# An adaLN block of cached attention and a gated MLP: loading order, first chunk and row stride of V changed

## The chip, the cores and the metric

One core of one Trainium2 chip runs the whole program. The metric is the time of one execution on the device in microseconds (us); a kernel's figure is the median of its runs. The profile comes from one execution, recorded instruction by instruction. The engines are called TensorE (PE for matmuls, PEld for weight loads), VectorE (DVE), ScalarE (ACT), GpSimd (POOL) and SyncE (SP, which here only issues DMAs). Each takes its instructions in the order in which the program issues them.

## The reference

Inputs are bfloat16: `x` (1, 2048, 512), a key and a value cache of 8 heads with 2048 rows of 128, 32 query heads (four to each key head), a spatial gating MLP of width 1792, and a modulation vector `c`.

```python
mod = (silu(c) @ w_mod).reshape(1, 6, 1, 512)
sa, ca, ga, sb, cb, gb = mod[:, 0], ..., mod[:, 5]
h = layernorm(x) * (1 + ca) + sa
q = (h @ wq) in 32 heads of 128
p = softmax(q k^T * 128 ** -0.5);  o = p v          # 4 query heads share a k/v head
x = x + ga * (o @ wo)
h = layernorm(x) * (1 + cb) + sb
z = gelu(h @ w_in);  z1, z2 = z[..., :896], layernorm(z[..., 896:])
g = w_sp @ z2 + b_sp                                # over the 2048 positions
x = x + gb * ((z1 * g) @ w_out)
```

## The kernel before

The order of all work is written out by hand: every engine gets its instructions in the order in which the Python code issues them, and waits are put in where data or a buffer asks for it. The function is `tile_adaLN_cond__gqa_block_cached__mixer_gmlp__prompt_kernel`.

**Units and slots.** Attention is cut into 128 units: unit u is key head u // 16 and query tile u % 16 (128 positions, four query heads, so 512 columns). The main loop runs over `it` (one unit each) and eight slots in it. In a slot `qk(it, i)` does two QK matmuls of 512 columns (L879) into a two-bank tile `s_ps`, and ScalarE makes the exponential of it, 1024 wide (L886). `pv(it - 1, i)` does eight PV matmuls of 129 columns (L901) for the unit before: 128 columns of V and a column of ones, which gives the softmax's sum. After slots 3 and 7 VectorE takes the reciprocal (L912) and scales (L913, `onorm`). Three units later `wo_proj` adds the output projection (L933) in slots 4 to 7, with a VectorE copy or add into `xacc` at the end.

**Order inside a slot.** First whatever was entered with `at(it, slot, fn)` into `later`, then `qk`, then `pv`, then the matmuls in `fill[it, slot]`, then one `wo_proj` matmul.

**Banks.** PSUM pools have two buffers of each name: `s_ps` (two banks each), `o_ps` (for PV and the modulation columns) and `misc` (one bank each; for query projections, output projections, transposes of layer-norm tiles, and the rows of the modulation). A buffer is given out again when the last user of its tile is done; a tile whose accumulation is still open keeps its buffer.

**Chunks.** Four tiles make a chunk of 512 positions. Before a chunk's queries can be projected, `ln1_stats` takes mean and variance of each tile on VectorE (L690, L691) and the reciprocal root on GpSimd (L671, L675), `ln1_norm` normalises (L679, VectorE), and `ln1_turn` transposes on TensorE (L796) in two halves, each into one `misc` bank, and evicts with scale and shift into `hT` (L803, VectorE). `qproj` multiplies with the query weights (L843) and casts into `qT` (L852, VectorE). `set_fill(b)` spreads the 16 projection matmuls of block b (a chunk for a key head) over slots.

**The beginning.** SyncE issues loads in the order c, tile 0 of x, the first third of `w_mod` (`wmod_a`), K of head 0, tiles 1 to 3 of x, the query weights of head 0, V of head 0, x tiles 4 to 7, the rest of `w_mod`, x tiles 8 to 15, `wo`, `w_in`. Then tile 0 is normalised, `mod_columns` makes shift and scale (L759), tile 0 is turned, K is transposed on TensorE (L821, 16 transposes) and copied by ScalarE in two halves (L825), and the queries of tile 0 are projected. Tiles 1 to 3 are normalised together (L829, L861), turned together at slot 0 of unit 0 and projected head by head with 384 columns over unit 0's eight slots (L1026 to L1029).

**Later chunks.** `ln1_at(it, ch)` enters chunk ch's statistics at slot 1, its normalisation at slot 5 and its turn at slot 7 of unit it: units 0, 2 and 5 for chunks 1, 2 and 3. `mod_rest` (L990) makes the other modulation columns and the gate rows (L1002) at slot 0 of unit 3. The projection of block 1 is spread over slots 0 to 7 of units 1 and 2, one matmul a slot; that of each later block over slots 0 to 3 of four units.

**V.** `load_v` puts V into tiles `v1` of 16 rows with `DV = DH + 8` = 136 elements each (272 bytes); the DMA writes 128 of them, GpSimd sets the others to one (L712), PV reads 129. The same `DV` sets the distance of the two heads in the `o_ps` bank.

Of the kernel before, what the change touches and what calls it, by code (L numbers as in the profile page):

```python
# [10 lines left out]
BF16 = mybir.dt.bfloat16  # L11
# [4 lines left out]
P = 128  # L16
# [559 lines left out]
def kernel(  # L576
# [19 lines left out]
    nc = tc.nc  # L596
    _, S, D = A_x.shape
    _, HKV, SK, DH = A_k_cache.shape
    HQ = A_wq.shape[1] // DH
    REP = HQ // HKV  # L600
# [5 lines left out]
    NDT = D // P  # L606
    NKT = SK // P
    NFT = FH // P
    NCH = S // 512
    CT = 512 // P  # L610
    FC = _f_chunk(FH)
    NFHC = FH // FC
    NSLOT = NKT // 2
    DV = DH + 8
    inv_sqrt_dh = 1.0 / math.sqrt(DH)

    NB = HKV * NCH
    x_dram = A_x[0].rearrange("(t p) d -> p t d", p=P)
# [4 lines left out]
    k_rows = A_k_cache[0].rearrange("g (p t) d -> p g t d", p=P)  # L623
# [18 lines left out]
    late = free_b.enter_context(tc.tile_pool(name="late", bufs=2, side="right"))  # L642
    early = free_a.enter_context(tc.tile_pool(name="early", bufs=2))

    x_sb = res.tile([P, NT, D], BF16, name="x_sb")
# [13 lines left out]
    ident = res.tile([P, P], BF16, name="ident")  # L659
    ones_bf = res.tile([P, P], BF16, name="ones_bf")  # L660

    def bank(name):
        return psum.tile([P, 512], FP32, name=name)

    def bank2():
        return psum.tile([P, 1024], FP32, name="s_ps")
# [28 lines left out]
    nc.sync.dma_start(out=c_bf[:], in_=c_dram)  # L695
    nc.sync.dma_start(out=x_sb[:, 0, :], in_=x_dram[:, 0, :])
    nc.sync.dma_start(out=wmod_a[:], in_=wmod_dram[:, :, 0 : 2 * D])
    k_nat = early.tile([P, SK], BF16, name="kT")
    nc.sync.dma_start(out=k_nat[:].rearrange("p (t d) -> p t d", d=DH), in_=k_rows[:, 0])
    nc.sync.dma_start(out=x_sb[:, 1:CT, :], in_=x_dram[:, 1:CT, :])  # L700

    groups, wqs, hTs, qTs = {}, {}, {}, {}

    def load_wq(g, engine):
        wqs[g] = early.tile([P, NDT, REP * DH], BF16, name="wq_g")
        engine.dma_start(
            out=wqs[g][:], in_=wq_dram[:, :, g * REP * DH : (g + 1) * REP * DH]
        )

    def load_v(g, rows, engine):  # L710
        v1 = late.tile([P, NKT, DV], BF16, name="v1")
        nc.gpsimd.memset(v1[:, :, DH:DV], 1.0)  # L712
        engine.dma_start(out=v1[:, :, 0:DH], in_=rows[:, g])
        groups[g]["v1"] = v1
# [11 lines left out]
    nc.gpsimd.memset(mhalf[:], -0.5)  # L726
    make_identity(nc, ident[:])
    load_wq(0, nc.sync)
    groups[0] = {}
    load_v(0, v_rows, nc.sync)  # L730
    nc.sync.dma_start(out=x_sb[:, CT : 2 * CT, :], in_=x_dram[:, CT : 2 * CT, :])
# [2 lines left out]
    load_wo(0, nc.sync)  # L734
    nc.sync.dma_start(out=win_sb[:], in_=win_dram)


    c_f = res.tile([P, NDT], FP32, name="c_f")
    nc.vector.tensor_copy(out=c_f[:], in_=c_bf[:])
# [6 lines left out]
    nc.vector.tensor_tensor(out=sc[:], in0=c_f[:], in1=sig[:], op=ALU.mult)  # L746
    sc_bf = res.tile([P, NDT], BF16, name="sc_bf")
    nc.vector.tensor_copy(out=sc_bf[:], in_=sc[:])
    nc.vector.memset(ones_bf[:], 1.0)

    def mod_columns(first, wmod, i0):

        mc_ps = bank("o_ps")
        for i in range(2):
            for dt in range(NDT):
                col = i * NDT + dt
                w0 = (first + i - i0) * D + dt * P
                for kt in range(NDT):
                    nc.tensor.matmul(  # L759
                        mc_ps[:, col : col + 1],  # L760
                        lhsT=wmod[:, kt, w0 : w0 + P],
                        rhs=sc_bf[:, kt : kt + 1],
                        start=(kt == 0),
                        stop=(kt == NDT - 1),
                    )
        c0 = first * NDT
        nc.vector.tensor_copy(out=modc[:, c0 : c0 + NDT], in_=mc_ps[:, 0:NDT])
        nc.vector.tensor_scalar_add(
            out=modc[:, c0 + NDT : c0 + 2 * NDT], in0=mc_ps[:, NDT : 2 * NDT], scalar1=1.0
        )  # L770


    def ln1_stats(j0, n):
        for j in range(j0, j0 + n):
            ln_stats(mv1, j, x_sb[:, j, :])
        return rstd_of(mv1[:, j0 : j0 + n, :], n, "ln1")

    def ln1_norm(j0, n, rstd):
        xns = []
        for j in range(j0, j0 + n):  # L780
            xn = res.tile([P, D], BF16, name="xn1", bufs=4)
            normalise(xn[:], x_sb[:, j, :], mv1[:, j, 0:1], rstd[:, j - j0 : j - j0 + 1])
            xns.append(xn)
        return xns

    def ln1_turn(j0, n, xns):
        ch, c0 = j0 // CT, (j0 % CT) * P
        if ch not in hTs:
            hTs[ch] = res.tile([P, NDT, 512], BF16, name="hT", bufs=NCH)
        hT = hTs[ch]  # L790
        for half in range(2):
            t_ps = bank("misc")[:].bitcast(BF16).rearrange("p (k q) -> p k q", k=2)
            for k in range(2):
                dt = half * 2 + k
                for jj in range(n):
                    nc.tensor.transpose(  # L796
                        t_ps[:, k, jj * P : (jj + 1) * P],
                        xns[jj][:, dt * P : (dt + 1) * P],
                        ident[:],
                    )  # L800
            for k in range(2):
                dt = half * 2 + k
                nc.vector.tensor_scalar(  # L803
                    out=hT[:, dt, c0 : c0 + n * P],
                    in0=t_ps[:, k, 0 : n * P],
                    scalar1=modc[:, NDT + dt : NDT + dt + 1],
                    scalar2=modc[:, dt : dt + 1],
                    op0=ALU.mult,
                    op1=ALU.add,
                )  # L810

    xns0 = ln1_norm(0, 1, ln1_stats(0, 1))
    mod_columns(0, wmod_a, 0)
    ln1_turn(0, 1, xns0)


    kT0 = early.tile([P, SK], BF16, name="kT")
    groups[0]["kT"] = kT0
    k_ps = bank2()[:].bitcast(BF16)
    for kt in range(NKT):  # L820
        nc.tensor.transpose(  # L821
            k_ps[:, kt * P : (kt + 1) * P], k_nat[:, kt * P : (kt + 1) * P], ident[:]
        )
    for hf in range(2):
        nc.scalar.copy(  # L825
            out=kT0[:, hf * SK // 2 : (hf + 1) * SK // 2],
            in_=k_ps[:, hf * SK // 2 : (hf + 1) * SK // 2],
        )
    rstd0 = ln1_stats(1, CT - 1)  # L829

    def qproj(b, heads, c0, n):

        g, ch = divmod(b, NCH)
        if b not in qTs:
            qTs[b] = early.tile([P, REP, 512], BF16, name="qT")
        one = n * len(heads) <= 512
        ps = {}

        def mm(hh, dt):
            if dt == 0 and (not one or hh == heads[0]):  # L840
                ps[0] = bank("misc")
            o0 = (hh - heads[0]) * n if one else 0
            nc.tensor.matmul(  # L843
                ps[0][:, o0 : o0 + n],
                lhsT=wqs[g][:, dt, hh * DH : (hh + 1) * DH],
                rhs=hTs[ch][:, dt, c0 : c0 + n],
                start=(dt == 0),
                stop=(dt == NDT - 1),
            )
            if dt == NDT - 1 and (not one or hh == heads[-1]):  # L850
                hs = heads if one else [hh]
                nc.vector.tensor_copy(  # L852
                    out=qTs[b][:, hs[0] : hs[-1] + 1, c0 : c0 + n],
                    in_=ps[0][:, 0 : len(hs) * n].rearrange("p (h q) -> p h q", q=n),
                )

        return [lambda hh=hh, dt=dt: mm(hh, dt) for hh in heads for dt in range(NDT)]

    for fn in qproj(0, list(range(REP)), 0, P):
        fn()  # L860
    xns0 = ln1_norm(1, CT - 1, rstd0)  # L861


    NU = HKV * NT
# [3 lines left out]
    def at(it, slot, fn):  # L868
        later.setdefault((it, slot), []).append(fn)
# [23 lines left out]
    def pv(u, i):  # L893
# [3 lines left out]
        if i % (2 * per) == 0:  # L897
            o_pss[u] = bank("o_ps")[:, 0 : 2 * DV].rearrange("p (h d) -> p h d", h=2)
        o_ps = o_pss[u]
# [116 lines left out]

    wsp = [None] * NCH

    def ln1_at(it, ch):
        st = {}  # L1020
        at(it, 1, lambda: st.update(r=ln1_stats(ch * CT, CT)))
        at(it, 5, lambda: st.update(x=ln1_norm(ch * CT, CT, st["r"])))
        at(it, 7, lambda: ln1_turn(ch * CT, CT, st["x"]))

    fill = {}
    rest0 = qproj(0, list(range(REP)), P, 512 - P)  # L1026
    at(0, 0, lambda: ln1_turn(1, CT - 1, xns0))
    for i in range(NSLOT):
        fill[0, i] = rest0[2 * i : 2 * i + 2]  # L1029
    ln1_at(0, 1)  # L1030
    ln1_at(2, 2)
    ln1_at(5, 3)
    at(3, 0, mod_rest)

    def set_fill(b):

        fs = qproj(b, list(range(REP)), 0, 512)
        for k, fn in enumerate(fs):
            it, slot = ((b - 1) * CT + k // NDT, k % NDT) if b > 1 else (1 + k // 8, k % 8)
            fill.setdefault((it, slot), []).append(fn)  # L1040

    def wsp0():
# [5 lines left out]
    for g in range(1, HKV):  # L1048
        it = (g - 1) * NT + 4
# [122 lines left out]
    for f in range(NFT):  # L1172
# [6 lines left out]
        out=ok1[:], in0=rall[:], scalar1=1.0 / SAFE, scalar2=None, op0=ALU.is_ge  # L1179
# [8 lines left out]
        out=bad[:], in0=okm[:], scalar1=-1.0, scalar2=1.0, op0=ALU.mult, op1=ALU.add  # L1188
# [133 lines left out]
```

## Time and profile before

| | us |
|---|---|
| median of three runs | 1346.97 (1346.54 to 1347.03) |
| the profiled execution | 1347.03 |
| its span, first to last instruction | 1345.2 |
| TensorE busy | 1303.1 (97%) |
| ScalarE busy | 1079.2 (80%) |
| VectorE busy | 476.3 (35%) |
| GpSimd busy | 46.4 (3%) |
| granted TensorE clock, mean over the span | 0.996 |

A row of the profile's groups gives line, engine, operation, what is written from what, the shapes, the count, then busy time in all with the mean length of one in ns, then the idle time of the engine ahead of it with what ended most of it. A row of the timeline gives start, length, engine, line, operation and, in brackets, idle time and its releaser. Two rows of the load times in the first 30 us: the query weights of head 0 landed 7.9 us after their issue at 3.28, and K 6.3 us after its issue at 2.26. VectorE's share is an average: in the first 45 us it runs short chains that other engines wait for.

### The profile page before, as it was taken

How to read it: one execution, taken by the hardware profiler on the slowest of the kernel's cores; microseconds unless marked ns; L12 is line 12 of the kernel's file. 1: busy time of each engine (PE TensorE's matmuls, PEld its weight loads, DVE VectorE, ACT ScalarE, POOL GpSimd, SP SyncE). 2: the span in 40 equal slices, each digit the busy share in tenths (PEclk: the TensorE clock that was granted, in tenths of full speed). 3: DMA queues.
4: the chain of work that ended last, by engine and by line, in shares of the span. 5: the costliest groups of instructions: out<-in, count | busy, mean ns of one | idle time of the engine just before them, and what ended most of it. 6: DMA issues, size and time to landing. Idle time of an engine off the chain costs nothing.

```text
span 1345.2 us, 27642 instructions
## 1 busy us (share of the span) xinstructions
PE 1303.1 (97%) x12137; PEld 860.4 (64%) x12345; DVE 476.3 (35%) x1171; ACT 1079.2 (80%) x1059; POOL 46.4 (3%) x88
## 2 busy tenths in 40 slices
PE   6999999999999999999999999999999999979997
PEld 4666666666666666666666666666666666534444
DVE  5442222222222222222222222222222666873344
ACT  4789999999999999999999999999999999540000
POOL 1010000000000000000000000000000000110000
PEclk9999999999999999999999999999999999989999
DMA  8120021102211120012010410121111111143200
GB/s 274 29 64 17 13 63 37 21 17 35 62 20 21 32 68 17 17 37 68 17 20 13 84 21 17 21 64 32 21 20 17 29 29 33 25 110 83 67 20 26
DMA packets 141184, 56.53 MB, mean 42 GB/s; under 512 B 131105, under 2 KB 136353, under 8 KB 141057
## 3 DMA queue, kind: packets, MB, share of 16 engines
q1 hardware_dynamic: 137504, 42.17, 15.0%
q0 software_dynamic: 3408, 12.45, 3.5%
q8 instruction: 98, 1.61, 0.5%
q14 instruction: 30, 0.24, 0.1%
q10 hardware_dynamic: 144, 0.07, 0.0%
HBM read 21.63 MB, written 2.10 MB: 18 GB/s over the span
## 4 chain that ended last, share of the span: by engine, by line
PE 92%; DVE 3%; SPq 2%; issue 1%; DMA 1%; POOL 0%; ACT 0%; ACTq 0%; POOLq 0%; DVEq 0%
PE s_ps L879 35%; PE o_ps L901 34%; PE misc L843 7%; PE misc L933 6%; PE misc L1205 6%; PE s_ps L1100 2%; SPq L1012 1%; PE o_ps L1220 1%; PE s_ps L1064 1%; DMA wq_g<-in_A_wq_dram 1%; DVE stz L1081 1%; DVE hT L803 0%; PE s_ps L1220 0%; PE misc L796 0%; DVE bnst L690 0%
## 5 line engine op out<-in xcount | busy, mean ns | idle before, releaser
L886 ACT ACTIVATE pT<-s_ps 128x1024 bf16<-128x1024 f32 x1024 | 1045.6, 1024 | 92.2 <-PE s_ps L879 16.5
L901 PEld LDWEIGHTS <-pT 128*128 128x128 bf16 x8192 | 548.5, 98 | 241.2
L901 PE MATMUL o_ps<-v,pT 128*128 128x129 bf16 x8192 | 631.4, 220 | 0.0
L879 PE MATMUL s_ps<-qT,kT 128*128 128x512 bf16 x2048 | 609.9, 379 | 10.8 <-DVE qT L852 0.8
L912 DVE RECIPROCAL rall<-o_ps 128x2 f32<-128x2 f32 x256 | 43.6, 170 | 750.9 <-PE o_ps L901 750.7
L879 PEld LDWEIGHTS <-kT 128*128 128x128 bf16 x2048 | 199.8, 98 | 120.1 <-issue 1.3
L843 PE MATMUL misc<-hT,wq_g 128*128 128x512 bf16 (+2 forms) x462 | 169.1, 376 | 0.8 <-DMA wq_g<-in_A_wq_dram 0.8
L933 PE MATMUL misc<-wo_g,oT 128*128 128x512 bf16 x386 | 146.3, 379 | 0.0
L913 DVE TENSOR_TENSOR onorm<-o_ps,rall 128x256 bf16<-128x256 f32 x256 | 108.7, 425 | 8.8
L1205 PE MATMUL misc<-wsp,z 128*128 128x512 bf16 (+2 forms) x555 | 100.5, 336 | 1.8 <-DVE gb L1214 1.3
L852 DVE CAST qT<-misc 128x512 bf16<-128x512 f32 (+1 forms) x129 | 87.2, 676 | 1.0 <-PE misc L843 1.0
L1205 PEld LDWEIGHTS <-z 128*128 128x128 bf16 x560 | 50.7, 98 | 50.3 <-issue 1.8
L946 DVE TENSOR_TENSOR xacc<-misc,xacc 128x512 f32<-128x512 f32 x112 | 76.2, 680 | 0.0
L843 PEld LDWEIGHTS <-wq_g 128*128 128x128 bf16 x528 | 51.8, 99 | 3.6 <-DMA wq_g<-in_A_wq_dram 1.0
L933 PEld LDWEIGHTS <-oT 128*128 128x128 bf16 x512 | 50.1, 98 | 0.7
L1214 DVE TENSOR_TENSOR gb<-misc,bsp_bc 128x512 bf16<-128x512 f32 (+2 forms) x35 | 20.4, 584 | 60.9 <-PE misc L1205 60.9
L1100 PE MATMUL s_ps<-hT,win_sb 128*128 128x512 bf16 x109 | 26.5, 401 | 7.3 <-ACT z1T L1108 7.1
L1108 ACT ACTIVATE z1T<-s_ps 128x1024 bf16<-128x1024 f32 x14 | 14.2, 1024 | 19.5 <-PE s_ps L1100 10.9
L1064 PE MATMUL s_ps<-win_sb,hT 128*128 128x448 bf16 x128 | 27.0, 352 | 0.1
L1074 ACT ACTIVATE z<-s_ps 128x896 bf16<-128x896 f32 x16 | 14.7, 917 | 14.9 <-PE s_ps L1064 14.9
L712 POOL MEMSET v<- 128x128 bf16 x8 | 1.6, 205 | 705.9 <-issue 606.9
L1100 PEld LDWEIGHTS <-win_sb 128*128 128x128 bf16 x112 | 11.5, 102 | 21.9 <-issue 10.1
(68 smaller groups left out, 288.6 us busy)
## 6 DMA issues: line engine op xcount, KB each, us to landing
v<-in_A_v_cache_dram POOLq DMA_DIRECT2D x7, 512.0 KB, 6.6
wo_g<-in_A_wo_dram POOLq DMA_DIRECT2D x7, 512.0 KB, 4.8
wq_g<-in_A_wq_dram POOLq DMA_DIRECT2D x7, 512.0 KB, 6.0
wsp<-in_w_mod_dram SPq DMA_DIRECT2D x1, 2048.0 KB, 9.2
oT<-onorm SPq DMA_TRANSPOSE x128, 2.4
out_dram<-yout SPq DMA_DIRECT2D x15, 128.0 KB, 1.7
win_sb<-in_B_w_in_dram SPq DMA_DIRECT2D x1, 1792.0 KB, 13.6
wmod_a<-in_w_mod_dram SPq DMA_DIRECT2D x1, 1024.0 KB, 5.4
```

The source lines that it names most:

```text
L843: nc.tensor.matmul(ps[0][:, o0 : o0 + n], lhsT=wqs[g][:, dt, hh * DH : (hh + 1) * DH], rhs=hTs[ch][:, dt, c0 : c0 + n], start=(dt == 0), s ...
L852: nc.vector.tensor_copy(out=qTs[b][:, hs[0] : hs[-1] + 1, c0 : c0 + n], in_=ps[0][:, 0 : len(hs) * n].rearrange("p (h q) -> p h q", q=n),)
L879: nc.tensor.matmul(s_ps[:, h * 512 : (h + 1) * 512].rearrange("p (r q) -> p r q", r=REP), lhsT=groups[g]["kT"][:, kt * P : (kt + 1) * P], ...
L886: nc.scalar.activation(out=pTs[u][:, 2 * i : 2 * i + 2, :], in_=s_ps[:].rearrange("p (k q) -> p k q", k=2), func=ACT.Exp, scale=inv_sqrt_dh,)
L901: nc.tensor.matmul(o_ps[:, hh % 2, 0 : DH + 1], lhsT=pTs[u][:, kt, hh * P : (hh + 1) * P], rhs=groups[g]["v1"][:, kt, 0 : DH + 1], start=( ...
L912: nc.vector.reciprocal(out=rall[:, c0 : c0 + 2], in_=o_ps[:, :, DH])
L913: nc.vector.tensor_tensor(out=onorms[u][:, hh - 1 : hh + 1, :], in0=o_ps[:, :, 0:DH], in1=rall[:, c0 : c0 + 2].unsqueeze(2).to_broadcast([ ...
L933: nc.tensor.matmul(X_ps[:], lhsT=oTs[u][:, hh, :], rhs=groups[g]["wo"][:, hh, :], start=(hh == 0), stop=(hh == REP - 1),)
L946: nc.vector.tensor_tensor(out=xaccs[j][:], in0=X_ps[:], in1=xaccs[j][:], op=ALU.add)
L1064: nc.tensor.matmul(ps[0][:, hf * 512 : hf * 512 + FC], lhsT=h2Ts[j // CT][:, dt, (j % CT) * P : (j % CT + 1) * P], rhs=win_sb[:, dt, FH + ...
L1100: nc.tensor.matmul(ps[0][:, k * 512 : (k + 1) * 512], lhsT=win_sb[:, dt, f * P : (f + 1) * P], rhs=h2Ts[2 * ch2 + k][:, dt, :], start=(dt ...
L1205: nc.tensor.matmul(g_ps[:, :n], lhsT=z2[:, st, f * P : (f + 1) * P], rhs=wsp[t][:, st, c0 : c0 + n], start=(st == 0), stop=(st == NT - 1),)
```

## The change

Five things are edited.

1. The loads: the query weights go ahead of K; K is loaded in two halves; tiles 1 to 3 of x follow them.
2. Idle matmuls: VectorE clears a tile of zeros first thing, and `warm(n)` issues n matmuls of 512 columns on it whose result nobody reads: 18 before the modulation columns, 3 behind them, 4 before the first query projection.
3. The first chunk: K's transposes and copies come after tile 0's query projection, in halves. Tiles 1, 2 and 3 are each handled by themselves, in units 0, 1 and 2: statistics at slot 0, normalisation at slot 1, turn at slot 2, and 16 projection matmuls of 128 columns, four in each of slots 4 to 7.
4. Later chunks: statistics at slot 4, normalisation at slot 7, turn at slot 0 of the next unit; `mod_rest` moves from slot 0 to slot 3 of unit 3; block 1's projection starts at slot 4 of unit 1 and ends at slot 3 of unit 3.
5. V's rows: `DV` is 130 in place of 136, so 260 bytes from row to row.

```diff
@@ -611,7 +611,7 @@
     FC = _f_chunk(FH)
     NFHC = FH // FC
     NSLOT = NKT // 2
-    DV = DH + 8
+    DV = DH + 2
     inv_sqrt_dh = 1.0 / math.sqrt(DH)
 
     NB = HKV * NCH
@@ -695,10 +695,6 @@
     nc.sync.dma_start(out=c_bf[:], in_=c_dram)
     nc.sync.dma_start(out=x_sb[:, 0, :], in_=x_dram[:, 0, :])
     nc.sync.dma_start(out=wmod_a[:], in_=wmod_dram[:, :, 0 : 2 * D])
-    k_nat = early.tile([P, SK], BF16, name="kT")
-    nc.sync.dma_start(out=k_nat[:].rearrange("p (t d) -> p t d", d=DH), in_=k_rows[:, 0])
-    nc.sync.dma_start(out=x_sb[:, 1:CT, :], in_=x_dram[:, 1:CT, :])
-
     groups, wqs, hTs, qTs = {}, {}, {}, {}
 
     def load_wq(g, engine):
@@ -726,6 +722,14 @@
     nc.gpsimd.memset(mhalf[:], -0.5)
     make_identity(nc, ident[:])
     load_wq(0, nc.sync)
+    k_nat = early.tile([P, SK], BF16, name="kT")
+    hk = NKT // 2
+    for hf in range(2):
+        nc.sync.dma_start(
+            out=k_nat[:, hf * SK // 2 : (hf + 1) * SK // 2].rearrange("p (t d) -> p t d", d=DH),
+            in_=k_rows[:, 0, hf * hk : (hf + 1) * hk],
+        )
+    nc.sync.dma_start(out=x_sb[:, 1:CT, :], in_=x_dram[:, 1:CT, :])
     groups[0] = {}
     load_v(0, v_rows, nc.sync)
     nc.sync.dma_start(out=x_sb[:, CT : 2 * CT, :], in_=x_dram[:, CT : 2 * CT, :])
@@ -734,6 +738,11 @@
     load_wo(0, nc.sync)
     nc.sync.dma_start(out=win_sb[:], in_=win_dram)
 
+
+
+    zeros = late.tile([P, REP, DH], BF16, name="onorm", bufs=3)
+    nc.vector.memset(zeros[:], 0.0)
+    nc.vector.memset(ones_bf[:], 1.0)
 
     c_f = res.tile([P, NDT], FP32, name="c_f")
     nc.vector.tensor_copy(out=c_f[:], in_=c_bf[:])
@@ -746,7 +755,15 @@
     nc.vector.tensor_tensor(out=sc[:], in0=c_f[:], in1=sig[:], op=ALU.mult)
     sc_bf = res.tile([P, NDT], BF16, name="sc_bf")
     nc.vector.tensor_copy(out=sc_bf[:], in_=sc[:])
-    nc.vector.memset(ones_bf[:], 1.0)
+
+    def warm(n):
+        w_ps = bank2()
+        for k in range(n):
+            nc.tensor.matmul(
+                w_ps[:, 0:512].rearrange("p (r d) -> p r d", r=REP), lhsT=zeros[:, 0, :], rhs=zeros[:], start=True, stop=True
+            )
+
+    warm(18)
 
     def mod_columns(first, wmod, i0):
 
@@ -811,22 +828,8 @@
 
     xns0 = ln1_norm(0, 1, ln1_stats(0, 1))
     mod_columns(0, wmod_a, 0)
+    warm(3)
     ln1_turn(0, 1, xns0)
-
-
-    kT0 = early.tile([P, SK], BF16, name="kT")
-    groups[0]["kT"] = kT0
-    k_ps = bank2()[:].bitcast(BF16)
-    for kt in range(NKT):
-        nc.tensor.transpose(
-            k_ps[:, kt * P : (kt + 1) * P], k_nat[:, kt * P : (kt + 1) * P], ident[:]
-        )
-    for hf in range(2):
-        nc.scalar.copy(
-            out=kT0[:, hf * SK // 2 : (hf + 1) * SK // 2],
-            in_=k_ps[:, hf * SK // 2 : (hf + 1) * SK // 2],
-        )
-    rstd0 = ln1_stats(1, CT - 1)
 
     def qproj(b, heads, c0, n):
 
@@ -856,9 +859,21 @@
 
         return [lambda hh=hh, dt=dt: mm(hh, dt) for hh in heads for dt in range(NDT)]
 
+    warm(4)
     for fn in qproj(0, list(range(REP)), 0, P):
         fn()
-    xns0 = ln1_norm(1, CT - 1, rstd0)
+
+
+    kT0 = early.tile([P, SK], BF16, name="kT")
+    groups[0]["kT"] = kT0
+    k_ps = bank2()[:].bitcast(BF16)
+    for hf in range(2):
+        for kt in range(hf * hk, (hf + 1) * hk):
+            nc.tensor.transpose(
+                k_ps[:, kt * P : (kt + 1) * P], k_nat[:, kt * P : (kt + 1) * P], ident[:]
+            )
+        half = slice(hf * SK // 2, (hf + 1) * SK // 2)
+        nc.scalar.copy(out=kT0[:, half], in_=k_ps[:, half])
 
 
     NU = HKV * NT
@@ -1016,27 +1031,32 @@
 
     wsp = [None] * NCH
 
-    def ln1_at(it, ch):
+    fill = {}
+    for jj in range(1, CT):
+        st1 = {}
+        at(jj - 1, 0, lambda jj=jj, st1=st1: st1.update(r=ln1_stats(jj, 1)))
+        at(jj - 1, 1, lambda jj=jj, st1=st1: st1.update(x=ln1_norm(jj, 1, st1["r"])))
+        at(jj - 1, 2, lambda jj=jj, st1=st1: ln1_turn(jj, 1, st1["x"]))
+        rest = qproj(0, list(range(REP)), jj * P, P)
+        for k, fn in enumerate(rest):
+            fill.setdefault((jj - 1, 4 + k // 4), []).append(fn)
+
+    def ln1_at(it, slot, ch):
         st = {}
-        at(it, 1, lambda: st.update(r=ln1_stats(ch * CT, CT)))
-        at(it, 5, lambda: st.update(x=ln1_norm(ch * CT, CT, st["r"])))
-        at(it, 7, lambda: ln1_turn(ch * CT, CT, st["x"]))
-
-    fill = {}
-    rest0 = qproj(0, list(range(REP)), P, 512 - P)
-    at(0, 0, lambda: ln1_turn(1, CT - 1, xns0))
-    for i in range(NSLOT):
-        fill[0, i] = rest0[2 * i : 2 * i + 2]
-    ln1_at(0, 1)
-    ln1_at(2, 2)
-    ln1_at(5, 3)
-    at(3, 0, mod_rest)
+        at(it, slot, lambda: st.update(r=ln1_stats(ch * CT, CT)))
+        at(it, slot + 3, lambda: st.update(x=ln1_norm(ch * CT, CT, st["r"])))
+        at(it + 1, 0, lambda: ln1_turn(ch * CT, CT, st["x"]))
+
+    ln1_at(0, 4, 1)
+    ln1_at(2, 4, 2)
+    ln1_at(5, 4, 3)
+    at(3, 3, mod_rest)
 
     def set_fill(b):
 
         fs = qproj(b, list(range(REP)), 0, 512)
         for k, fn in enumerate(fs):
-            it, slot = ((b - 1) * CT + k // NDT, k % NDT) if b > 1 else (1 + k // 8, k % 8)
+            it, slot = ((b - 1) * CT + k // NDT, k % NDT) if b > 1 else (1 + (k + 4) // 8, (k + 4) % 8)
             fill.setdefault((it, slot), []).append(fn)
 
     def wsp0():
```

## The prediction

> **What bounds the kernel now.** I read four views: the page's groups of instructions, the busy time by stretches, the chain of waits over the first 80 us, and TensorE's timeline around the unit boundaries.
>
> ```profile
> L886 ACT ACTIVATE pT<-s_ps 128x1024 bf16<-128x1024 f32 x1024 | 1045.6, 1024 | 92.2 <-PE s_ps L879 16.5
> L901 PE MATMUL o_ps<-v,pT 128*128 128x129 bf16 x8192 | 631.4, 220 | 0.0
> L879 PE MATMUL s_ps<-qT,kT 128*128 128x512 bf16 x2048 | 609.9, 379 | 10.8 <-DVE qT L852 0.8
> ```
> ```profile
> 400.00:1100.00 700.00, 693.75 (x6877) 474.99 (x6996) 209.61 (x527) 651.05 (x637) 16.28 (x28) 1.00 0.16 32
> ```
>
> The second fence holds, behind the stretch and its length, the busy time of PE, PEld, DVE, ACT and POOL. TensorE is busy 693.75 of 700 us there, and nothing in the change shortens this part. What it can move is the beginning, and every idle moment of TensorE that it adds or takes away up to the last edited unit.
>
> ```profile
> 3.28 7.95 DMA wq_g<-in_A_wq_dram
> 11.23 0.05 issue
> 11.28 1.90 PE misc L843 x16
> ...
> 20.80 1.05 POOL rstd_ln L675
> 21.85 0.03 issue
> 21.88 1.38 DVE xn L679 x4
> 23.26 0.48 DVE qT L852
> ...
> 27.66 0.60 PE s_ps L879 x2
> ```
>
> Here the chain (start, length, what) shows the beginning waiting for the query weights, then for the statistics of chunk 1 (VectorE, then GpSimd, then VectorE), then for the last query cast. QK of unit 1 starts at 27.66.
>
> ```profile
> 43.96 0.38 PE L843 MATMUL misc<-hT,wq_g 128*128 128x512 bf16 x1
> 44.18 0.61 PE L796 MATMUL misc<-ident,xn 128*128 128x128 bf16 x8
> 45.88 0.62 PE L796 MATMUL misc<-ident,xn 128*128 128x128 bf16 x8 [1.09 <-DVE hT L803]
> 46.34 0.59 PE L879 MATMUL s_ps<-qT,kT 128*128 128x512 bf16 x2
> 46.77 0.62 PE L901 MATMUL o_ps<-v,pT 128*128 128x129 bf16 x8
> 47.44 0.94 PE L759 MATMUL o_ps<-sc_bf,wsp 128*128 128x1 bf16 x32
> 49.02 1.90 PE L1002 MATMUL misc<-wsp,lhs_bc 128*128 128x512 bf16 x8 [0.64 <-DVE lhs_bc L995]
> 50.76 0.59 PE L879 MATMUL s_ps<-qT,kT 128*128 128x512 bf16 x2
> ```
>
> This is chunk 2's turn at slot 7 of unit 2: an open query head holds one of the two "misc" banks, both halves share the other, and TensorE waits 1.25 from the issue end of one half to the other (1.09 shown, after the pipeline's 0.165). The same follows at 76.97 for chunk 3. With 0.64 at L1002, idle time from unit 1 to unit 7 is 3.14.
>
> **Durations used,** all from this timeline. TensorE queue time: 512 columns 0.215, 128 columns 0.056 at the full clock (8 in 0.61 with the tail) and 0.107 at the slow one (L821, 16 in 1.89). QK with PV is 0.88 a slot, 1.10 with one 512-column matmul. VectorE: statistics 0.80 a tile, normalise 0.33 each in a row and 0.41 alone, hT eviction 0.47 for 512 columns and 0.27 for 128, reciprocal 0.20, onorm 0.36, cast 0.60 in a row, 0.69 to its end. GpSimd from the last statistic: 1.0 for one tile, 1.45 for four. Exps run every 0.92 in unit 0. Following each queue in program order with these, the old code gives QK of units 1, 2, 3, 4 at 27.7, 36.5, 50.7, 58.7, against 27.66, 36.47, 50.76, 58.76 in the trace.
>
> **The head, step by step.** Loads land in the order of issue. Moved behind wmod_a, wq takes K's place: K landed at 2.26 + 6.3 = 8.6, with the same 512 KB. K's halves then land at 9.4 and 10.1, x 1-3 at 11.2 (as many bytes ahead as wq had); the extra issue costs SP 0.50, and V and x 4-7 keep their bytes ahead (13.5, 14.95). So wq's 11.23 leaves the path. The 18 idle matmuls start near 1.2, behind a memset. All slow they end at 1.2 + 18 x 0.427 = 8.9, all fast at 5.1; the weights land at 7.27, so they cost 0 to 1.6. I take 0.3 (two thirds slow), since the old clock got fast (QK pairs from 0.97 to 0.59 near 18) under a load with gaps. Then: modulation columns 7.6 to 8.6, three idle matmuls 0.65, four transposes 9.5, four evictions to 10.6 (four idle matmuls fit below them), query projection to 11.5, cast to 12.2. K's transposes follow it; its copies, 0.965 each (L825), end near 12.95 and 13.85. Exp 0 starts at 13.9, not 17.05: 3.1 earlier.
>
> By the Trainium skill ("TensorE: Matmul & The Clock Gate", Part 1, the HAM clock gate) the clock opens after a busy window of 3.4 us, free-running; an estimate from it ends the idle matmuls between 6.8 and 8.9, which agrees with my end points; the old trace needed some 10 us from its first matmul.
>
> **Unit 0** no longer follows its exps. VectorE does tile 1's statistics (12.2 to 13.0; GpSimd to 14.05), normalise, evictions to 15.9, then chunk 1's statistics, 4 x 0.80 to 19.2, GpSimd to 20.65, four normalisations, and only behind these in its queue the cast of tile 1's queries, 22.0 to 22.65. The second half of chunk 1's turn waits for that cast's bank, and QK of unit 1 waits behind the turn: 23.15. The exps alone would allow 21.2. **Gain at this point: 27.70 - 23.15 = 4.55.**
>
> **Units 1 to 6: what is added.** Tiles 2 and 3 of chunk 0, which lay before unit 1, now each cost 4 transposes and 16 projections, 20 x 0.056 = 1.12; two make **2.24**. These units have no slack on TensorE, so this counts in full. The row behind it: 128-column transposes and 129-column PV matmuls, each with its own weight load, run at 0.056. The skill's page ("Back-to-back issue gap") gives about 81 ns for such pairs at 128 columns, which speaks against cutting 384 columns into 128; by it the 32 projections would cost 0.8 more. The row decides.
>
> **New idle time of TensorE:**
> - (1,2), turn of tile 2: its statistics (queued behind tile 1's cast), GpSimd, and chunk 1's four evictions lie ahead of its normalisation: 0.77.
> - (2,0): the cast of tile 2's queries stands on VectorE behind reciprocal and onorm; TensorE runs one 512-column matmul and waits 1.07. At (3,0) this lies within the next wait but one.
> - (2,2), turn of tile 3: its norm is late by 0.63, then an open head leaves one bank and the halves wait for each other, 0.82: 1.45. A further 0.18 at slot 4.
> - (3,0), chunk 2: statistics at slot 4, normalise at slot 7. Statistics 3.2 and GpSimd 1.45 fill the time to slot 7's end, 1.3 of normalisation comes after, and reciprocal, onorm and both casts are queued behind it; the turn needs their banks: 3.20 (was 1.25).
> - (3,3), the rest of the modulation, moved into an open head: L1002 waits 0.59 for its left sides, and the second four wait 0.94 for the first copy out of the single free bank: 1.53 (was 0.64).
> - (6,0), chunk 3: the same order; 2.8 for the normalised tiles, 0.89 for the xacc add's bank: 3.69 (was 1.25).
>
> Sum 11.9, against 3.14 before: **+8.76**. The rest of the program issues what it did.
>
> **Rows of V** at 260 bytes rather than 272. No row shows such a stride. PV's 56.4 ns already lies on the line through 128 columns (56) and 512 (215.5), 0.415 ns a column and 2.8 fixed, so nothing is to be won. QK's moving operand comes in four separate pieces at the same rate, which is the nearest row, so I take 0; the bound above is a second fixed part per matmul, 8192 x 2.8 ns = 22.9. V's first load (2.3 by landing times) could be slower; twice as slow it would hold x 4-7 until 17.2 and cost 1.3. Later V loads have a whole group's time.
>
> **Sum:** -4.55 + 2.24 + 8.76 = +6.45. The profiled execution ran 1347.03 with a span of 1345.2; 1351.65 + 1.83 is 1353.5, and the median lies 0.06 lower: **1353.4**.
>
> **Rivals.**
> - *The chunk turns cost no more than before; not slower.* Statistics, GpSimd and normalisation are 5.95 together, slots 4 to 7 take 4.4 to 5.3. Started some 1.6 us sooner, or covered, they would fit, and 1.95 + 0.89 + 2.44 = 5.3 falls away: +1.2, 1348.1. If the tile waits (3.3) vanish as well, 1344.8. For it: VectorE is 35% busy. Against: it takes its queue in order, and in the old trace chunk 2's statistics began at 37.60, with their slot (37.57). It decides from a stall sum below 8 us. 0.19.
> - *The idle matmuls don't do their work.* They end at 8.9, 1.3 later than taken, and the clock falls back in unit 0, 0.8 by the slow rows: 1355.5. For it: unit 0's first slots use TensorE 0.43 of 0.92. 0.13.
> - *V's stride costs TensorE* one column a matmul, 8192 x 0.415 ns = 3.4: 1356.8. It decides from any PV group over 0.455 for 8. Against: the pieces of QK. 0.10.
>
> **How the numbers follow.** My forecast has 0.58. One bank choice better than I assume takes off up to 2.8 (0.82 + 0.15 + 0.94 + 0.89): 1350.6. The late idle matmuls, the clock and V's load add 3.4: 1356.8; the stride's tail and a little of the first rival widen this to 1349.8 to 1357.8. A measurement here tells 0.2% (2.7 us) from no change. Slower 0.81 (forecast and the last two rivals); the first rival gives 0.12 to the same and 0.07 to faster.
>
> **What would show it.** wq landing near 8.6 and exp 0 near 14; QK of unit 1 near 23; gaps before L796 of 3 us or more at (3,0) and (6,0), behind L679; two waits at L1002; PV groups still 0.45. I am wrong if unit 7 starts before its old time (87), or if PV's spacing moved.

## The result, and the profile after

The changed kernel took 1371.83 us (1371.03 to 1373.06, four runs) against 1347.00 in the same comparison: 1.0182 times the time before, interval 1.0164 to 1.0199, so 24.8 us slower. The direction was forecast, the size was not: 1353.4 was expected, and the range ended at 1357.8.

The page's groups, with the same columns as before:

```profile
L901 ACT ACTIVATE pT<-s_ps 128x1024 bf16<-128x1024 f32 x1024 | 1045.7, 1025 | 114.6 <-PE s_ps L894 39.4
L916 PE MATMUL o_ps<-v,pT 128*128 128x129 bf16 x8192 | 646.9, 220 | 0.0
L894 PE MATMUL s_ps<-qT,kT 128*128 128x512 bf16 x2048 | 608.9, 379 | 12.6 <-DVE qT L855 0.9
```

PV (now L916) is busy 646.9 in place of 631.4 us, with the same 8192 matmuls and the same 220 ns each. The length of one matmul hides it, since matmuls overlap in the pipeline; what grew is the distance between two starts (table below). QK (now L894) did not grow.

The busy time by stretches (PE, PEld, DVE, ACT, POOL, clock, DMA share, GB/s), for the middle of the program and for two places near its beginning:

```profile
400.00:1100.00 700.00, 693.69 (x6789) 476.82 (x6906) 198.57 (x497) 642.71 (x629) 13.62 (x22) 1.00 0.16 31
```
```profile
48.00:50.00 2.00, 0.55 (x6) 0.54 (x6) 1.97 (x5) 0.00 (x0) 0.00 (x0) 0.76 0.77 188
50.00:52.00 2.00, 2.00 (x16) 1.45 (x14) 1.49 (x4) 0.00 (x0) 0.00 (x0) 0.50 0.98 139
...
86.00:88.00 2.00, 1.33 (x13) 1.04 (x11) 1.80 (x5) 0.00 (x0) 0.00 (x0) 0.64 0.80 291
88.00:90.00 2.00, 2.00 (x12) 1.31 (x11) 0.93 (x2) 1.02 (x1) 0.00 (x0) 0.50 0.94 268
```

In the middle TensorE is as busy as before, 693.69 of 700, yet ScalarE makes fewer exponentials in the same time (629 instructions in place of 637): busy, and slower. The second fence shows something else, a granted clock of one half at two places where nothing of the kind stood before.

The chain of waits over the beginning:

```profile
1.78 5.30 DMA wmod_a<-in_w_mod_dram
...
14.94 1.10 DVE hT L820 x4
16.04 0.61 DVE bnst L690
...
19.64 1.06 POOL rstd_ln L675
20.73 1.38 DVE xn L679 x4
22.11 0.60 DVE qT L855
```

The query weights are gone from it; it runs through the modulation weights, tile 1's evictions and chunk 1's statistics, then the cast behind the normalisation. The timeline of TensorE at the boundary of units 2 and 3:

```profile
45.32 0.60 PE L846 MATMUL misc<-hT,wq_g 128*128 128x128 bf16 x5
49.45 1.87 PE L813 MATMUL misc<-ident,xn 128*128 128x128 bf16 x16 [3.53 <-DVE qT L855]
51.11 1.06 PE L894 MATMUL s_ps<-qT,kT 128*128 128x512 bf16 x2
51.97 0.85 PE L916 MATMUL o_ps<-v,pT 128*128 128x129 bf16 x8
```

After 3.53 us of waiting the 16 transposes take 1.87 and a QK pair 1.06, in place of 0.59: the slow clock, seen in the work itself.

The starts of the units, by their first QK matmul, tell where the 24 us lie:

```
unit             0      1      2      3      4      7      64      127
before         16.0   27.7   36.5   50.8   58.8   87.3   589.3   1141.7
after          12.9   23.2   34.1   51.1   64.8   97.7   606.3   1165.7
difference     -3.0   -4.5   -2.3   +0.4   +6.0  +10.4   +16.9    +24.0
```

Up to unit 7 the change costs 10.4; over the 120 units behind it, where only V's rows differ, another 13.6 comes slot by slot: about 14 ns in each of 960 slots (a slot holds eight PV matmuls).

### The profile page after: what moved, and what is told of

Same layout as the page of the kernel before. It is cut to its first block, busy times and chain, and to the rows that moved or that the text cites. A ratio compares the mean times of both kernels' runs of the same rounds, so it can differ in the third digit from the quotient of the medians.

```text
span 1369.2 us, 27771 instructions
## 1 busy us (share of the span) xinstructions
PE 1325.5 (97%) x12193; PEld 877.3 (64%) x12402; DVE 478.7 (35%) x1179; ACT 1079.3 (79%) x1059; POOL 47.0 (3%) x92
## 4 chain that ended last, share of the span: by engine, by line
PE 91%; DVE 4%; SPq 1%; issue 1%; POOL 1%; DMA 1%; ACT 0%; ACTq 0%; POOLq 0%; DVEq 0%
PE o_ps L916 35%; PE s_ps L894 34%; PE misc L948 7%; PE misc L846 6%; PE misc L1225 6%; PE s_ps L1120 2%; SPq L1027 1%; PE o_ps L1240 1%; DVE bnst L690 1%; PE s_ps L1084 1%; DVE stz L1101 1%; DVE xn L679 0%; DMA wmod_a<-in_w_mod_dram 0%; PE s_ps L1240 0%; PE misc L813 0%
## 5 line engine op out<-in xcount | busy, mean ns | idle before, releaser
L916 PEld LDWEIGHTS <-pT 128*128 128x128 bf16 x8192 | 560.3, 98 | 242.4 <-issue 1.1
L916 PE MATMUL o_ps<-v,pT 128*128 128x129 bf16 x8192 | 646.9, 220 | 0.0
L894 PE MATMUL s_ps<-qT,kT 128*128 128x512 bf16 x2048 | 608.9, 379 | 12.6 <-DVE qT L855 0.9
L894 PEld LDWEIGHTS <-kT 128*128 128x128 bf16 x2048 | 196.5, 96 | 123.0 <-issue 3.3
L948 PE MATMUL misc<-wo_g,oT 128*128 128x512 bf16 x444 | 167.5, 377 | 0.0
L846 PE MATMUL misc<-hT,wq_g 128*128 128x512 bf16 (+1 forms) x437 | 146.0, 355 | 0.0
L855 DVE CAST qT<-misc 128x512 bf16<-128x512 f32 x128 | 87.0, 681 | 1.0 <-PE misc L846 1.0
L1094 ACT ACTIVATE z<-s_ps 128x896 bf16<-128x896 f32 x16 | 14.7, 917 | 15.0 <-PE s_ps L1084 15.0
```

The costliest lines, as they stand in the source:

```text
L846: nc.tensor.matmul(ps[0][:, o0 : o0 + n], lhsT=wqs[g][:, dt, hh * DH : (hh + 1) * DH], rhs=hTs[ch][:, dt, c0 : c0 + n], start=(dt == 0), s ...
L855: nc.vector.tensor_copy(out=qTs[b][:, hs[0] : hs[-1] + 1, c0 : c0 + n], in_=ps[0][:, 0 : len(hs) * n].rearrange("p (h q) -> p h q", q=n),)
L894: nc.tensor.matmul(s_ps[:, h * 512 : (h + 1) * 512].rearrange("p (r q) -> p r q", r=REP), lhsT=groups[g]["kT"][:, kt * P : (kt + 1) * P], ...
L916: nc.tensor.matmul(o_ps[:, hh % 2, 0 : DH + 1], lhsT=pTs[u][:, kt, hh * P : (hh + 1) * P], rhs=groups[g]["v1"][:, kt, 0 : DH + 1], start=( ...
L948: nc.tensor.matmul(X_ps[:], lhsT=oTs[u][:, hh, :], rhs=groups[g]["wo"][:, hh, :], start=(hh == 0), stop=(hh == REP - 1),)
```

## The experiments

Ratios are to the kernel before, each with its 95% interval.

**V's rows alone.** From the kernel before:

```diff
-    DV = DH + 8
+    DV = DH + 2
```

> The kernel before with DV = 130 alone (V rows 260 bytes apart, o_ps heads 520 bytes apart). Theory A (V's rows off a 16-byte boundary cost TensorE in every PV matmul; in the changed kernel PV matmuls at positions 0 and 4 of a group of eight start 56.6 and 55.8 ns before the next, the others 59.2 to 60.9): eight cost 15 to 17 ns more, over 1024 groups about +16 us, so 1362 to 1364, and PV groups of 0.47 in place of 0.453. Theory B (the 14 us that the head and the chunk turns do not explain come from a rearrangement of the order that slows every slot): 1346 to 1348.

1362.29 (ratio 1.0104, 1.0087 to 1.0121), +14.7. The rows alone cost more than half of the loss.

**Everything but V's rows.** From the changed kernel:

```diff
-    DV = DH + 2
+    DV = DH + 8
```

> The changed kernel with DV = 136, so everything but the V rows. Theory A: the rest of the change costs what the two traces show up to unit 7, about +10.4 (6.45 of the forecast, some 3.4 from two windows of 3.4 us at half the clock after long waits, 0.7 from chunk 2's normalisation being slower beside a V load): 1356.5 to 1358. Theory B: about 1371.

1358.11 (1.0077, 1.0060 to 1.0094), +10.5. The two parts add up: 14.65 + 10.47 = 25.1, against 24.8 measured together. Theory B falls. This run's trace has a third stretch at half the clock, from 22.9 to 26.3 us, which the changed kernel's trace does not have; it matters below.

**Reading V, or writing o_ps.** `DV` sets both. From the kernel before, with only V's tile narrowed:

```diff
-        v1 = late.tile([P, NKT, DV], BF16, name="v1")
-        nc.gpsimd.memset(v1[:, :, DH:DV], 1.0)
+        v1 = late.tile([P, NKT, DH + 2], BF16, name="v1")
+        nc.gpsimd.memset(v1[:, :, DH : DH + 2], 1.0)
```

> The kernel before with V rows of 130 elements, but the two heads in the o_ps bank left 136 apart (544 bytes). Theory A (reading V in SBUF is what costs): as v_only, 1362 to 1364. Theory C (writing o_ps at 520 bytes, or VectorE reading it there, is what costs): 1346 to 1348.

1362.71 (1.0108, 1.0091 to 1.0125). So the cost lies with V's tile and not with `o_ps`; theory C falls. That it lies in reading the tile is settled by the order of reading, below.

**264 bytes.** From the kernel before, `DV = DH + 4`:

> The kernel before with DV = 132: rows 264 bytes apart, so every second row starts on a multiple of 16 bytes and the others 8 past it. Theory A with a boundary of 16 bytes: every second PV matmul costs about 3 ns more, 8192 x 1.5 ns = +10 to +13 us, 1357 to 1360, with a period of two inside a group. If 8 bytes are enough: 1346 to 1348. If it is any stride but a multiple of 16 that costs every matmul: 1362 or more.

1354.82 (1.0050, 1.0034 to 1.0067), +7.2, half of v_only's loss, and with a period of two. It is less than I expected, since part of each delay is made up by the matmuls behind it: in the table below the distance after a slow one is 55.8 ns in place of 56.7.

**Start of a row, or distance between rows.** From the kernel before, rows still 272 bytes apart, V four elements further on:

```diff
-        nc.gpsimd.memset(v1[:, :, DH:DV], 1.0)
-        engine.dma_start(out=v1[:, :, 0:DH], in_=rows[:, g])
+        nc.gpsimd.memset(v1[:, :, 4 + DH : DV], 1.0)
+        engine.dma_start(out=v1[:, :, 4 : 4 + DH], in_=rows[:, g])
...
-                rhs=groups[g]["v1"][:, kt, 0 : DH + 1],
+                rhs=groups[g]["v1"][:, kt, 4 : DH + 5],
```

> The kernel before, V rows still 272 bytes apart (136 elements), but V and its ones column stored 4 elements further, so that every row that PV reads starts 8 bytes past a multiple of 16. If the start of the row counts: every PV matmul pays what the odd ones paid at 264 bytes, (503.0 - 493.6) / 4 = 2.4 ns, 18.8 ns a group, +19 us: 1364 to 1369, with no period in a group. If the distance between rows counts, not their start: 1346 to 1349.

1347.74 (1.0002, 0.9993 to 1.0012): nothing. So theory A, as I had put it, is wrong: rows that start 8 bytes off a multiple of 16 are free as long as their distance is 272. A row holds 258 bytes that are read. At 260, counting rows from 0, rows 1, 2 and 3 of every four begin in the 16 bytes in which the row before them ends; at 264 every second one does; at 272, shifted or not, none does. That became theory F, and two runs tried it.

**The same rows, read downwards.** From v_only:

```diff
-        for kt in range(part * NKT // per, (part + 1) * NKT // per):
+        for kt in reversed(range(part * NKT // per, (part + 1) * NKT // per)):
...
-                start=(kt == 0),
-                stop=(kt == NKT - 1),
+                start=(kt == NKT // per - 1),
+                stop=(kt == NKT - NKT // per),
```

> v_only (rows 260 bytes apart, 1362.3) with the eight PV matmuls of a group taken from the last row of V to the first. v_shift showed that the start of a row alone costs nothing. Theory F: a matmul pays when its first element lies in the same 16 bytes as the last element of the matmul before it in time (at 260: rows 1, 2, 3 of every four, with row 4 starting a new 16 bytes; at 264 every second row; at 272 none, shifted or not). Going down, no row starts where the one before it in time ended, so nothing is paid: 1346 to 1349, PV spacing 56.7 throughout. Theory G: what counts is how a row lies in memory beside its neighbours, in whatever order: 1361 to 1364.

1348.62 (1.0004, 0.9995 to 1.0014). With the same tile and the same bytes, the order in which the rows are read takes the 14 us away (the weights from `pT` are taken in that order too; reading downwards at 272 was not run). Theory G falls.

**280 bytes.** From the kernel before, `DV = DH + 12`:

> The kernel before with DV = 140, rows 280 bytes apart: again no multiple of 16, every second row starting 8 past one, but with 22 bytes between a row's last element and the next row's start, so that no two rows share 16 bytes. Theory F: 1346 to 1349. Theory H (any distance that is no multiple of 16 costs): as v_264, 1353 to 1356, with a period of two.

1348.10 (1.0001, 0.9991 to 1.0011). Theory H falls.

The distance from each PV matmul's start to the next one's, in ns, worked out from the starts in the traces (groups of eight between 150 and 1000 us that the next matmul follows at once), with the sum of the eight:

```
                 1     2     3     4     5     6     7     8     sum
before  (272)  56.7  56.7  56.7  56.7  56.7  56.7  56.7  56.7  453.3
v_shift (272)  56.7  56.7  56.7  56.7  56.7  56.7  56.6  56.7  453.3
v_only  (260)  56.5  60.8  59.2  59.2  55.8  59.4  59.3  59.4  469.7
after   (260)  56.5  60.9  59.2  59.2  55.8  59.3  59.3  59.4  469.6
v_264          56.7  60.8  55.8  59.3  55.8  59.4  55.8  59.2  462.9
v_280          56.7  59.2  55.8  56.1  55.8  58.8  55.8  56.5  454.8
v_260_down     56.7  56.7  56.7  56.7  60.0  55.8  55.8  55.8  454.2
```

The slow places of 260 and 264 are those that theory F names: 2, 3, 4 and 6, 7, 8 at 260, every second one at 264. It does not name the single slow places of the last two rows (2 and 6 at 280, 5 downwards), which cost 0.8 to 1.4 ns a group, most of it made up at once; what those are stays open. The rows also fix the 16: with 8 bytes in its place 264 would be free, and with 32 every second row at 272 would pay, and neither is so. That two matmuls in a row meet in the same 16 bytes is the rule that fits all the large delays of the seven rows; the mechanism behind it was not seen. A group of v_only is 16.4 ns longer while a slot is only 14 ns longer: the 512-column matmuls of the slot start the next one after 215.0 to 215.4 ns there, after 215.8 in the kernel before.

**Chunk statistics earlier.** From all_but_v; each line gives the unit and slot of a chunk's statistics, normalisation and turn, and the turns stay where they are:

```diff
-    ln1_at(0, 4, 1)
-    ln1_at(2, 4, 2)
-    ln1_at(5, 4, 3)
+    ln1_at((0, 4), (0, 7), (1, 0), 1)
+    ln1_at((1, 5), (2, 4), (3, 0), 2)
+    ln1_at((5, 0), (5, 5), (6, 0), 3)
```

> all_but_v (the changed kernel with DV = 136, 1358.1) with chunk 2's statistics moved from slot 4 of unit 2 to slot 5 of unit 1, its normalisation from slot 7 to slot 4 of unit 2, and chunk 3's statistics and normalisation from slots 4 and 7 of unit 5 to slots 0 and 5; the turns stay. Theory D (the waits ahead of the two turns, and the two stretches of 3.4 us at half the clock that follow them, are most of the +10.5): 2.0 at chunk 2, 2.8 at chunk 3, 3.4 of clock and 0.7 of the slow normalisation go: 1348 to 1351, no stretch at half the clock between 20 and 1000 us. Theory E (tiles handled one by one cost most, the chunk turns little): 1355 or more.

1348.92 (1.0010, 1.0000 to 1.0019), 1.5 above the kernel before: some 9 of the 10.5 us are gone. Two rows of TensorE's timeline, at chunk 2's and chunk 3's turn, hold in brackets what is left of the waits:

```profile
46.91 1.21 PE L813 MATMUL misc<-ident,xn 128*128 128x128 bf16 x16 [0.88 <-DVE qT L855]
...
79.75 0.61 PE L813 MATMUL misc<-ident,xn 128*128 128x128 bf16 x8 [0.65 <-DVE xacc L959]
```

In all_but_v the waits there were 3.39 and, at chunk 3, 3.13 in four pieces; they have become 0.88 and 0.65, and the granted clock stays at one from 6 to 1183 us. Theory E falls: the tiles handled one by one are not what costs most. The waits, the clock and the slower normalisation went together here; no run separates them.

**Without the idle matmuls.** From all_but_v, the three calls of `warm` taken out:

> all_but_v without its 25 idle matmuls. If they raise the clock: full clock only near 18 us as in the kernel before, in place of 4.7, the first query projection and K's 16 transposes at 107 ns each in place of 56 (about 0.8 each), QK of unit 1 0.5 to 2 us later than 23.4, and the time 1358 to 1360. If they do nothing: the same trace from 12 us on.

1359.21 (1.0087, 1.0071 to 1.0104), not told apart from all_but_v's 1.0060 to 1.0094. The traces say a little more. The clock opens at 12.3 us in place of 5.9 (18 was expected), and the first QK starts at 13.72 in place of 13.16. Unit 1 starts at 23.99, against 23.79 in all_but_v and 23.20 and 23.49 in the changed kernel and chunks_early, which have the idle matmuls too. So they open the clock sooner, and that is worth 0.2 to 0.8 us at unit 1. The comparison with all_but_v is not clean, since all_but_v alone has the slow stretch from 22.9 to 26.3 us:

```profile
21.42 2.58 PE L813 MATMUL misc<-ident,xn 128*128 128x128 bf16 x16 [0.67 <-DVE xn L679]
23.79 1.06 PE L894 MATMUL s_ps<-qT,kT 128*128 128x512 bf16 x2
```

**A version from these readings.** DV = 136 and the changed kernel's head; tiles 1 to 3 together again; each chunk's turn in two halves, in slots where one bank is free; statistics well ahead; the rest of the modulation moved out of the crowded units; block 1's projection begun three slots later. From all_but_v, the new lines without those that they replace:

```diff
+    at(0, 0, lambda: st0.update(r=ln1_stats(1, CT - 1)))
+    at(0, 1, lambda: st0.update(x=ln1_norm(1, CT - 1, st0["r"])))
+    at(0, 3, lambda: ln1_turn(1, CT - 1, st0["x"]))
+    for k, fn in enumerate(qproj(0, list(range(REP)), P, 512 - P)):
+        fill.setdefault((0, 4 + k // 4), []).append(fn)
...
+        for half in range(2):
+            at(*t[half], lambda half=half: ln1_turn(ch * CT, CT, st["x"], (half,)))
...
+    ln1_at((1, 0), (1, 4), ((1, 5), (1, 6)), 1)
+    ln1_at((2, 1), (2, 7), ((3, 1), (3, 3)), 2)
+    ln1_at((5, 0), (5, 6), ((6, 1), (6, 3)), 3)
+    at(9, 0, mod_rest)
...
+            it, slot = ((b - 1) * CT + k // NDT, k % NDT) if b > 1 else (1 + (k + 7) // 8, (k + 7) % 8)
```

> DV = 136 and the changed kernel's head (load order, idle matmuls, K behind the first projection), but tiles 1 to 3 together in unit 0 as in the kernel before (turn at slot 3, 384-column projections in slots 4 to 7), chunk turns with their halves in two slots where a bank is free, statistics five or more slots ahead of normalisation's end, the rest of the modulation at slot 0 of unit 9, block 1's projection from slot 7 of unit 1. By the queue-by-queue sums that gave the changed kernel's unit 1 at 23.15: 4.6 below the kernel before, 1341 to 1344. If the waits only move elsewhere: 1347 or more.

1343.55 (0.9969, 0.9956 to 0.9981): faster than both, and in the range that was expected. What each of its edits gives was not measured by itself. In its timeline the turns of chunks 2 and 3 are met without a wait:

```profile
43.00 0.61 PE L813 MATMUL misc<-ident,xn 128*128 128x128 bf16 x8
45.65 0.61 PE L813 MATMUL misc<-ident,xn 128*128 128x128 bf16 x8
71.12 0.61 PE L813 MATMUL misc<-ident,xn 128*128 128x128 bf16 x8
73.77 0.61 PE L813 MATMUL misc<-ident,xn 128*128 128x128 bf16 x8
```

## Why the prediction was right in sign and wrong in size

**The step that failed: "Rows of V ... so I take 0".** It measured +14.7. The nearest row I chose, QK's moving operand in four separate pieces, has pieces that lie far apart, so it could not show what happens when one read ends where the next begins. The bound from above, 22.9 (a second fixed part of 2.8 ns in every matmul), held for the sum but not for the reason given: three of four matmuls pay 2.5 to 4.2 ns, some of them more than 2.8, and the total stays below because every fourth pays nothing and part is made up. I then left it out of the range, and priced the rival that named it at 3.4 us, one column a matmul, with nothing to support that size. The forecast had named PV's spacing as a sign of being wrong, and it moved: from 56.7 ns (56.4 in the prediction is the line's value) to 58.7 on average. A cost with bounds of 0 and 22.9 on 8192 instructions of the bounding engine belongs in the range.

**The head held.** Exp 0 was expected at 13.9 and came at 14.04; QK of unit 1 at 23.15 and came at 23.20, a gain of 4.46 where 4.55 was forecast. The cause was the one named: chunk 1's statistics and the cast behind its normalisation.

**The new waits held, each at its place.** The trace's brackets leave out the 0.165 us of matmul tail that my figures hold, so with that taken off: (1,2) 0.52 for 0.61; (2,0) 0.88 for 0.91; (2,2) 0.64 + 0.69 for 1.12; (3,0) 3.53 for 3.04; (3,3) 0.49 + 0.78 for 1.20. At (6,0), with the tails, 4.0 in five pieces for 3.69. By these terms the front was to be still ahead at unit 3, by about 1; it was behind by 0.4.

**What the sum of idle time left out.** Up to unit 7 the loss was 10.4, not 6.45. The clock fell after the two long waits: two stretches of 3.41 us at one half, 49.0 to 52.4 and 86.6 to 90.0, in which TensorE worked some 3 us each and so lost about 1.5 each (an estimate: half of the work in them). I had counted waits as if the work after them ran at its old speed; only the head's clock was bounded. V's slower groups make up 0.7 by then, and chunk 2's normalisation took 0.7 longer (below). With the forecast's 6.45 that is 10.9, 0.5 more than measured, so one of these is somewhat smaller.

By the Trainium skill ("TensorE: Matmul & The Clock Gate", Why this matters for your kernels) idle gaps of more than about 3 us put the array back to half its clock. The traces agree in part. One gap of 3.53 was followed by the half clock, and the waits of up to 1.1 in the kernel before were not. But chunk 3's wait was broken by eight transposes, its longest piece 1.97. In all_but_v the slow stretch at 22.9 follows waits of 0.67 and about 1, and in v_shift, whose beginning is that of the kernel before, one follows waits of 0.88, 1.09 and 0.80, the last two of the same length as in the kernel before:

```profile
25.58 0.62 PE L796 MATMUL misc<-ident,xn 128*128 128x128 bf16 x8 [1.09 <-DVE hT L803]
26.04 0.59 PE L879 MATMUL s_ps<-qT,kT 128*128 128x512 bf16 x2
26.47 0.49 PE L843 MATMUL misc<-hT,wq_g 128*128 128x384 bf16 x2
27.75 0.98 PE L879 MATMUL s_ps<-qT,kT 128*128 128x512 bf16 x2 [0.80 <-DVE qT L852]
28.53 1.07 PE L901 MATMUL o_ps<-v,pT 128*128 128x129 bf16 x8
```

In the 3.41 us before that stretch TensorE was busy 1.52 us; in the kernel before it was busy 1.51 in the same 3.4 us of work and kept the full clock. So a single gap of 3 us is not needed, and what decides between two such executions is not shown here. On that point the measurement decides. I used the page for the head alone.

**Rivals.** The first (turns no dearer than before) was wrong for the change as made, and right about its condition: with the statistics begun earlier, chunks_early came to 1348.9 where it had 1348.1. The second did not occur in the changed kernel: the 18 idle matmuls were over by 7.1, the modulation columns began at 7.13, and the clock stayed open. With the same head all_but_v did fall back, at 22.9, so that this rival's second half was kept away by luck. The third happened, four times as large as priced.

## What to carry to other kernels

Where an operand of many short matmuls is laid out in rows, look at where one read ends and the next begins, in time order: here a read that began in the 16 bytes in which the one before it ended cost 2.5 to 4.2 ns, 1% of the time in all; rows far enough apart not to meet cost nothing, and the narrow rows read downwards nothing that could be measured. When statistics, a second engine and a normalisation are put into consecutive slots, add up their durations against the slots' time, and list what is queued behind the last of them on the same engine. A stretch in which the bounding engine mostly waits is to be priced with the slow clock that may follow it: 3.41 us at one half in these traces, some 1.5 us of work lost each time.

## What the runs showed of the hardware that was not expected

**Meeting ends.** A PV matmul that begins in the 16 bytes where the one before it ended starts the next one 59 to 61 ns later in place of 56.7. The Trainium skill ("SBUF — State Buffer", Specifications) has 16-byte cachelines with a penalty for each access that crosses to a new line. Counted from their addresses, the 258 bytes of every row in these runs lie in 17 such lines, whatever the distance, so that a penalty per line would charge all the forms alike. The runs show a cost for coming back to the same line with the next instruction, of which the page says nothing, and none for rows that start off a boundary (v_shift).

**GpSimd's loads beside VectorE.** The four normalisations of a chunk take 1.37 to 1.38 us where GpSimd is idle, 1.91 to 1.92 where it issues V's load at the same time (2.10 to 2.25 with V's rows 260 bytes apart), and 1.63 where it issues those of `wo` and the query weights (chunk 3 of the changed kernel). Two rows of the changed kernel:

```profile
46.15 1.40 POOL L709 DMA_DIRECT2D v<-in_A_v_cache_dram  x1
46.17 2.10 DVE L679 TENSOR_SCALAR xn<-x_sb,mv,rstd_ln 128x512 bf16<-128x512 bf16 x4 [1.49 <-POOL rstd_ln L675]
```

The load stands at slot 3 of unit 5 in the code, but nothing in GpSimd's queue waits for that, so it is issued as soon as chunk 2's root is done; the later place of chunk 3's statistics let it slip in front, beside a normalisation that TensorE was waiting for. That the load slows the normalisation is read from these times; no run separated it.
